# Fourteen tiles of the attention backward turned by DMA instead of by TensorE, with the buffers and the order that this needs

## The chip, the cores and the metric

The kernel runs on one NeuronCore of a Trainium2 chip. The metric is the device time of one execution in microseconds (us), from the profiler's clock. Three executions of the kernel before took 904.92, 905.37 and 907.75 us; their median is 905.37 us.

## The reference

What is computed is the forward output and all weight and input gradients of a gated mix of two branches on a sequence of 2048 tokens of width 512: `A`, attention with 32 heads of width 16 and a sliding window of 256 tokens, and `B`, a gated feed-forward of width 1376.

```python
g = sigmoid((x * gate_w).sum(-1, keepdims=True))
# A: qkv = x @ wqkv; scores = q k^T / 4, masked to 0 <= i - j < 256; p = softmax; o = p v
a = (o transposed back) @ wo
# B: gate = x @ W_gate; up = x @ W_up; gate = gate * (gate > 0)
b = (gate * up) @ W_down
out = g * a + (1 - g) * b
# returned: out, and by jax.vjp with grad_out the gradients of
# x (through A alone), wqkv, wo, W_gate, W_up, W_down, gate_w
```

All inputs and outputs are bfloat16.

## The kernel before

**Three stages.** The first (0 to about 250 us of the profile) is the feed-forward with its weight gradients. The second (250 to about 705 us) is the attention, forward and backward in one pass; the change lies here. The third (705 to 905 us) has two loops over the 16 token tiles: first the products with `W_down` and the gradient of `wo`, then the gradient of `x` and the output.

**Units of the attention.** The 32 heads are four *head groups* `c` = 0 to 3 of eight heads. The 2048 tokens are 16 tiles `j` of 128 queries, in four *token groups* `tg` of four tiles. A query tile sees three key tiles `kb`: its own (role `d`, masked along the diagonal), the one before (role `m`, unmasked) and the one two before (role `f`, the *far* tile, masked the other way). Four heads at a time (`half` 0 holds the even heads, `half` 1 the odd ones) make one *unit*: a 128 x 512 tile of probabilities. A head group has 90 units, all four have 360.

For each unit TensorE makes `ST` (line 688: scores of four heads, 128 x 512) and `dPT` (line 711: gradient of the probabilities). ScalarE takes the exponential of `ST` (line 697), GpSimd masks it if the role is `d` or `f`, and VectorE multiplies it with `dPT` (line 716). This gives two tiles, `Pu` and `Pd`. `rowsum` (lines 725 and 727) multiplies both, as they are, into `BA`. The products `CD` (`cd_piece`, lines 542 and 545), which give the gradients of the keys and values, need `Pu` and `Pd` *turned* (transposed in blocks of 128 x 128).

**How a unit is turned.** `flip` does it in one of two ways. Roles `d` and `m` are turned by DMA: the two halves of a tile lie in one buffer (`PPd`, `PPm`), and one DMA transpose from the queue of SyncE (SP) turns both, 128 x 2048 elements (line 744). Far units (and four `m` units at the end) are turned by TensorE: eight 128 x 128 transposes against the identity into `pt` (line 754), and then one copy of 128 x 1024 out of PSUM by ScalarE or VectorE, by turns (line 72 or 74; the tile is named `p`).

**The order of the work** is written out by hand: a loop over slots `n`, one unit entering in each. In slot `n` the kernel emits `ST` and the exponential of unit `n`, `dPT` of unit `n-1`, the product of VectorE for unit `n-2`, the DMA turn of unit `n-3`, and `rowsum` of unit `n-4` with its turn on TensorE, if it has one. Inside a slot, other work fills in:

- `cdq` holds the `CD` products with the slot from which each may run. When all units of query tile `j` are through `rowsum`, the six products of key tile `j-2` enter: those of older query tiles may run one slot later, those of tile `j` itself (the far units) five slots later. The queue is worked strictly in order.
- `prq` holds the six steps of `project_parts` for the next token group: projections Q and dO, the turn of these two by DMA (`rows`, line 181, 128 x 1024 elements), projections K and V, and `tr_kv`. A running `credit` (1.5 for a slot, less what each step costs) and a slot by which it is due decide when a step is emitted.
- `bgq` holds 16 pieces of `grad_parts`: the weight gradient of the head group before (line 642), four matmuls each, four pieces in a row to one PSUM tile. They enter at query tile 3 of the next head group, all together.
- `late` holds weight loads for the third stage (`plan`): among them the turns of `wqkv` by DMA (line 582) into the slot `p0`, after the projections of the fifth token group. `W_rest` is the list of the other weight turns for the third stage: four are issued at the end of the attention, one more at each pair of token tiles in the first loop of the third stage.

K and V (`K0`, `K1`, `V0`, `V1`, `KV1`) of a token group are read by the units of this group and of the first two query tiles of the next. Three sets of buffers hold them: one in the pool `pjA`, two in the pool `pj` (line 126 and line 519).

SP's queue, in order, issues the DMA turns of the attention, the stores of weight gradients (`ws`) and of `rows_st` (line 565), and the loads.

Of the kernel before, what the change touches and what calls it, by code (L numbers as in the profile page):

```python
# [11 lines left out]
BF = mybir.dt.bfloat16  # L12
# [10 lines left out]
def kernel(  # L23
# [20 lines left out]
    nc = tc.nc  # L44
    P = 128
# [9 lines left out]
    NT = S // P  # L55
# [42 lines left out]
    def slot(tag):  # L98
        return big.tile([P, DC, TGW], BF, tag=tag, name=tag)
# [12 lines left out]
    if True:  # L112
# [10 lines left out]
        def project_parts(c, tg):  # L123
            t4 = {}
            proj[(c, tg)] = t4
            pj = lambda: pjA if (c * NTG + tg) % 3 == 0 else pjs["b"]

            def mm(nm, which, eng):
                ps, tag, bufs, _, _ = pools["now"]
# [385 lines left out]
    if True:  # L515
        st = p3.enter_context(tc.tile_pool(name="attst", bufs=2))
        gwp = p3.enter_context(tc.tile_pool(name="gwp", bufs=2))
        p3b = ExitStack()
        pjs["b"] = p3b.enter_context(tc.tile_pool(name="pj", bufs=2))
        wk = p3b.enter_context(tc.tile_pool(name="attw", bufs=2))  # L520
        pps = ExitStack()
        ps = pps.enter_context(tc.tile_pool(name="attps", bufs=2, space=PSUM))
# [61 lines left out]
        def clear(name):  # L584
            nc.gpsimd.memset(W6[(name, FC - 1)][0:FC * P - F, :], 0.0)
# [32 lines left out]
        def load_gw():  # L618
            nc.sync.dma_start(gw_b[:], gate_w.partition_broadcast(P))

        plan = {2: [load_gw], 5: turns("wqkv", A_wqkv, 0, 4, "p0"), 7: turns("wqkv", A_wqkv, 4, 8, "p1"),
                11: turns("wqkv", A_wqkv, 8, 12, "p2"),
                12: turns("Wg", B_W_gate, 0, 4, "x0") + turns("Wg", B_W_gate, 4, 8, "d0"),
                15: loads("Wd", B_W_down, 0, "x3") + loads("Wd", B_W_down, 4, "d3") + loads("Wd", B_W_down, 8, "p3")}
        W_rest = (turns("Wg", B_W_gate, 8, 12, "x1") + [lambda: clear("Wg")] + turns("Wu", B_W_up, 0, 4, "d1") + turns("Wu", B_W_up, 4, 8, "x2")
                  + turns("Wu", B_W_up, 8, 12, "d2") + [lambda: clear("Wu")])

        def grad_parts(c, tail=False):
            out = []
# [26 lines left out]
                    out.append((lambda part=part, t0=t0, f=(t0 == 0), l=(t0 + 4 == NT): piece(part, t0, f, l), t0 + 4 < NT))  # L656
            return out

        class Unit:
            pass  # L660

        units = []
        for c in range(DC):
            for j in range(NT):
                kbs = [k for k in (j - 1, j, j - 2) if k >= 0]
                for half in range(2):
                    order = kbs if half or len(kbs) < 3 else [kbs[0], kbs[2], kbs[1]]
                    for ki, kb in enumerate(order):
                        u = Unit()
                        u.c, u.j, u.kb, u.half = c, j, kb, half  # L670
                        u.first = ki == 0 and half == 0
                        u.last = ki == len(kbs) - 1 and half == 1
                        u.role = ("d", "m", "f")[j - kb]
                        u.pair = u.role == "d" or (u.role == "m" and (c < DC - 1 or j < NT - 2))
                        u.own = u.role == "f"
                        u.dma = u.pair
                        units.append(u)
        NU = len(units)

        pairs = {}  # L680

        def front(u):
            tg, jl = u.j // TPG, u.j % TPG
            z = zt[(u.c * NTG + tg) % ZB]
            KTt = proj[(u.c, u.kb // TPG)][f"K{u.half}"]
            ksl = slice((u.kb % TPG) * P, (u.kb % TPG + 1) * P)
            ST = ps.tile([P, HH, P], F32, tag="M", bufs=4, name="ST")
            nc.tensor.matmul(ST[:], lhsT=KTt[:, ksl], rhs=z[:, 0, :, jl, :], start=True, stop=True)  # L688
            if not u.own:
                if u.half == 0:  # L690
                    tag = f"PP{u.role}"
                    pairs[(u.c, u.j, u.kb)] = wk.tile([P, 2, 2, HH, P], BF, tag=tag, bufs=3, name=tag)
                u.PP = pairs[(u.c, u.j, u.kb)][:, u.half, :, :, :]
                u.Pu, u.Pd = u.PP[:, 0, :, :], u.PP[:, 1, :, :]
            else:
                u.Pu = wk.tile([P, HH, P], BF, tag="Pu", bufs=2, name="Pu")
            nc.scalar.activation(u.Pu[:], ST[:], ACT.Exp)  # L697
            if u.role == "d":
                nc.gpsimd.affine_select(out=u.Pu[:], in_=u.Pu[:], compare_op=ALU.is_ge, fill=0.0, base=0,  # L699
                                        pattern=[[0, HH], [1, P]], channel_multiplier=-1)  # L700
            elif u.role == "f":
                nc.gpsimd.affine_select(out=u.Pu[:], in_=u.Pu[:], compare_op=ALU.is_ge, fill=0.0, base=-1,  # L702
                                        pattern=[[0, HH], [-1, P]], channel_multiplier=1)
# [7 lines left out]
            nc.tensor.matmul(u.dPT[:], lhsT=VTt[:, ksl], rhs=z[:, 1, :, jl, :], start=True, stop=True)  # L711

        def gradp(u):
            if u.own:
                u.Pd = wk.tile([P, HH, P], BF, tag="Pd", bufs=2, name="Pd")
            nc.vector.tensor_tensor(out=u.Pd[:], in0=u.Pu[:], in1=u.dPT[:], op=ALU.mult)  # L716

        def rowsum(u):
# [17 lines left out]
        def flip(u):  # L736
            key = (u.c, u.j, u.kb, "p2")
            if u.role != "f" and key not in P2 and not (u.pair and u.half == 0):
                P2[key] = wk.tile([P, 2, 2, HH, P], BF, tag=f"P2{u.role}", bufs=3, name=f"p2{u.role}")
            if u.dma:  # L740
                if u.pair and u.half == 0:
                    return
                hs = slice(0, 2) if u.pair else slice(u.half, u.half + 1)
                nc.sync.dma_start_transpose(out=P2[key][:, hs, :, :, :].rearrange("p b a h q -> p (b a h) q"),
                                            in_=pairs[(u.c, u.j, u.kb)][:, hs, :, :, :].rearrange("p b a h q -> p (b a h q)"))
                for b in range(2)[hs]:
                    P2[(u.c, u.j, u.kb, b)] = P2[key][:, b, :, :, :]
                return
            eng = ("act", "dve", "act")[copier["i"] % 3] if u.c == 0 else ("act", "dve")[copier["i"] % 2]
            copier["i"] += 1  # L750
            pt = psr.tile([P, 2, HH, P], BF, tag="TR", name="pt")
            for a, src in enumerate((u.Pu, u.Pd)):
                for hh in range(HH):
                    nc.tensor.transpose(pt[:, a, hh, :], src[:, hh, :], ident[:])  # L754
            p2 = P2[key][:, u.half, :, :, :] if u.role == "m" else wk.tile([P, 2, HH, P], BF, tag="P2f", bufs=4, name="p2")[:]
            evac(p2, pt[:], eng)
            P2[(u.c, u.j, u.kb, u.half)] = p2

# [84 lines left out]
        with tc.manual_schedule():  # L843
# [36 lines left out]
            while n <= NU + LAG or ev or cdq or bgq:  # L880
                now = ev.pop(n, [])
                u = units[n] if n < NU else None
                if u is not None:
                    gi = u.c * NTG + u.j // TPG
                    if u.first and u.j == 0:
                        sts[u.c] = st.tile([P, NT, 4, P], BF, tag="rows_st", name="rows_st")
                    if u.first and u.j % TPG == 0:
                        if gi + 1 < len(groups):
                            prq = project_parts(*groups[gi + 1]) if gi else second
                            due = n + sum(2 * min(3, j + 1) for j in range(u.j, u.j + TPG)) - 3  # L890
                            if gi + 2 == len(groups):
                                due -= 10
                    if u.first and u.j == TPG and ends:
                        copies.append(ends.pop(0))
                    if u.first and u.j == 1 and u.c > 0:
                        ready = grad_parts(u.c - 1)
                    if u.first and u.j == TPG - 1 and u.c > 0:
                        bgq += ready
                    front(u)
                    if u.last and gi + 1 == len(groups) and u.j % TPG in (1, 3):  # L900
                        ev.setdefault(n + 2, []).append(("dma", (lambda: load_a(0)) if u.j % TPG == 3 else lambda: load_h(0)))
# [18 lines left out]
                if w is not None:  # L920
                    rowsum(w)
                    if not w.dma:
                        flip(w)
                    if w.last:
                        for s, eng, f in small_ops(w.c, w.j, n - 2):
                            ev.setdefault(s, []).append((eng, f))
                        done = [w.j - 2] if w.j >= 2 else []
                        if w.j == NT - 1:
                            done += [NT - 2, NT - 1]
                        for kb in done:  # L930
                            qbs = range(kb, min(NT, kb + 3))
                            for qb in qbs:
                                for half in range(2):
                                    e = n + (1 if qb < w.j else 5)
                                    cdq.append((e, w.c, kb, qb, half, qb == qbs[-1] and half == 1))
                if v is not None and not (w is not None and w.first):
                    front_dp(v)
# [13 lines left out]
                elif held and credit > 0.3:  # L951
                    held = background()
                    credit -= 0.65
                elif prq and not held and ((credit > 0.4 and n > fed + 1) or due - n <= len(prq)):
                    fed = n
                    credit -= (0.44, 0.86, 0.86, 0.1, 0.86, 0.86)[len(prq) - 1]
                    prq.pop(0)()
# [3 lines left out]
                        ev.setdefault(n + 1, []).append(("dma", flush))  # L961
                    if not prq:
                        late += plan.get(gi + 1, [])
                elif bgq and len(prq) <= 2 and credit > 0.3:
                    held = background()
                    credit -= 0.65
                if u is not None and u.c == DC - 1 and not bgq and u.j > 6 and "grads" not in S2:
# [179 lines left out]
```

## Time and profile before

| | |
|---|---|
| median of three executions | 905.37 us |
| profiled execution: its time | 907.23 us |
| profiled execution: its span | 905.5 us |
| TensorE (PE) busy | 889.8 us, 98% of the span |
| VectorE (DVE), ScalarE (ACT), GpSimd (POOL) busy | 510.8, 445.6, 493.9 us |
| mean granted TensorE clock | 0.998 |
| turns of far units and others on TensorE (line 754) | 928 transposes (448 from `Pu`, 448 from `Pd`, 32 from `PPm`) |
| DMA turns (line 744) | 64 of `PPd`, 58 of `PPm` |

The span runs from the first to the last instruction of the core; the execution's time has some 1.7 us more around it. Matmuls overlap in the array, so the busy time of a line of TensorE, a sum of durations, is more than the time that it takes of the engine; what a matmul costs is read from the distance of the starts in the timeline.

### The profile page before, as it was taken

Reading aid. Unit: us, or ns where it says so; the run is one execution under the profiler, and the core shown is the slowest. Engines: PE = TensorE matmul, PEld = TensorE weight load, DVE = VectorE, ACT = ScalarE, POOL = GpSimd, SP = SyncE. Lnnn points to the kernel's source line nnn. Section 1 sums busy time; section 2 is a strip of 40 time slices with the busy share of each in tenths; the row PEclk is TensorE's granted clock in tenths of the full one; section 3 lists DMA queues with packets and bytes.
Section 4 is the critical chain, followed back from the end, with each engine's and each line's share of the span. In section 5 each row is a group of like instructions: output and inputs, shape, how many; then the busy total and the mean of one; then the engine's idle time right before and its main releaser. Section 6 shows DMA issues by size and latency. Waiting matters only on the chain.

```text
span 905.5 us, 25948 instructions
## 1 busy us (share of the span) xinstructions
PE 889.8 (98%) x10607; PEld 561.2 (62%) x10607; DVE 510.8 (56%) x946; ACT 445.6 (49%) x787; POOL 493.9 (55%) x937
## 2 busy tenths in 40 slices
PE   8999999999989999999999999999998999999998
PEld 5565665665657777667776677766676544444445
DVE  4433435434468887678886778876787101433343
ACT  6422223222278777667776677766787212111111
POOL 3654445445267778767877577876687200222232
PEclk9999999999999999999999999999999999999999
DMA  9989889999889999999999989999999999998940
GB/s 300 188 183 200 190 189 203 214 220 212 193 143 159 185 185 198 186 169 155 181 176 192 183 162 187 173 196 184 199 207 193 226 234 241 261 273 218 203 121 30
DMA packets 520984, 174.57 MB, mean 193 GB/s; under 512 B 446817, under 2 KB 519745, under 8 KB 520865
## 3 DMA queue, kind: packets, MB, share of 16 engines
q1 hardware_dynamic: 498624, 150.62, 89.6%
q10 hardware_dynamic: 20608, 17.70, 7.3%
q0 software_dynamic: 1632, 4.59, 1.4%
q8 instruction: 83, 1.36, 0.6%
q14 instruction: 37, 0.30, 0.1%
HBM read 34.37 MB, written 36.24 MB: 78 GB/s over the span
## 4 chain that ended last, share of the span: by engine, by line
PE 86%; DVE 5%; POOL 2%; ACT 2%; DMA 2%; issue 1%; SPq 1%; ACTq 0%; POOLq 0%; DVEq 0%
PE wps L412 8%; PE dxps L1049 8%; PE ST L688 7%; PE dPT L711 7%; PE pt L754 5%; PE dxps L1079 4%; PE gps L363 4%; PE dhps L363 4%; PE dps L414 4%; PE ups L363 4%; PE bps L1026 4%; PE pp L133 4%; PE BA L725 4%; PE CD L542 4%; PE wps L642 4%; PE BA L727 2%
## 5 line engine op out<-in xcount | busy, mean ns | idle before, releaser
L688 PE MATMUL ST<-z,K 128*128 128x512 bf16 x360 | 135.8, 378 | 3.3 <-ACT PPd L697 1.3
L711 PE MATMUL dPT<-z,V 128*128 128x512 bf16 x360 | 135.9, 378 | 1.8 <-DVE Pd L716 0.5
L699 POOL TENSOR_SCALAR_AFFINE_SELECT PPd<-PPd 128x512 bf16<-128x512 bf16 x128 | 81.7, 638 | 79.6 <-ACT PPd L697 79.3
L377 POOL TENSOR_TENSOR hT<-rg,upm 128x512 bf16<-128x512 bf16 x44 | 51.3, 1166 | 114.4 <-DVE upm L375 103.6
L412 PE MATMUL wps<-dgu_r,x_r 128*128 128x256 bf16 (+1 forms) x704 | 103.9, 270 | 0.0
L716 DVE TENSOR_TENSOR PPd<-PPd,dPT 128x512 bf16<-128x512 bf16 x128 | 86.9, 680 | 19.9 <-PE dPT L711 12.3
L702 POOL TENSOR_SCALAR_AFFINE_SELECT Pu<-Pu 128x512 bf16<-128x512 bf16 x112 | 72.3, 646 | 35.3 <-ACT Pu L697 34.2
L697 ACT ACTIVATE PPd<-ST 128x512 bf16<-128x512 f32 x128 | 77.0, 602 | 23.7 <-PE ST L688 18.8
L716 DVE TENSOR_TENSOR Pd<-Pu,dPT 128x512 bf16<-128x512 bf16 x112 | 76.4, 682 | 21.6 <-PE dPT L711 11.3
L412 PEld LDWEIGHTS <-x_r 128*128 128x128 bf16 x704 | 68.4, 98 | 30.8
L697 ACT ACTIVATE Pu<-ST 128x512 bf16<-128x512 f32 x112 | 67.4, 602 | 37.2 <-PE ST L688 37.1
L716 DVE TENSOR_TENSOR PPm<-PPm,dPT 128x512 bf16<-128x512 bf16 x120 | 80.1, 667 | 7.1 <-PE dPT L711 5.9
L697 ACT ACTIVATE PPm<-ST 128x512 bf16<-128x512 f32 x120 | 72.4, 603 | 17.2 <-PE ST L688 16.7
L375 DVE SCALAR_TENSOR_TENSOR upm<-rg,ups 128x512 bf16<-128x512 bf16 x44 | 30.1, 684 | 79.9 <-PE ups L363 42.1
L369 ACT ACTIVATE rg<-gps 128x512 bf16<-128x512 f32 x44 | 26.3, 597 | 88.8 <-PE gps L363 53.8
L414 PE MATMUL dps<-db_r,h_r 128*128 128x512 bf16 x176 | 66.7, 379 | 0.0
L72 ACT COPY p<-pt 128x1024 bf16<-128x1024 bf16 x59 | 60.1, 1019 | 4.2
L1061 ACT COPY a_sb<-aps 128x512 f32<-128x512 f32 x16 | 9.4, 586 | 106.9 <-issue 99.8
L387 POOL TENSOR_TENSOR dgu<-dh_sb,rg 128x512 bf16<-128x512 bf16 x44 | 57.9, 1315 | 5.3 <-ACT dh_sb L383 5.3
L642 PE MATMUL wps<-rows_st,x_r 128*128 128x384 bf16 x256 | 50.3, 325 | 0.0
L386 DVE TENSOR_TENSOR dgu<-dh_sb,upm 128x512 bf16<-128x512 bf16 x44 | 33.0, 749 | 29.9 <-ACT dh_sb L383 27.0
L133 PE MATMUL pp<-x,p 128*128 128x512 bf16 x192 | 49.0, 377 | 0.0
(178 smaller groups left out, 2327.9 us busy)
## 6 DMA issues: line engine op xcount, KB each, us to landing
dqkvo_d<-rows_st SPq DMA_DIRECT2D x15, 512.0 KB, 3.9
hT_d<-hT ACTq DMA_DIRECT2D x44, 128.0 KB, 2.8
dgT_d<-dgu ACTq DMA_DIRECT2D x44, 128.0 KB, 3.1
duT_d<-dgu ACTq DMA_DIRECT2D x44, 128.0 KB, 2.9
h<-hT_d SPq DMA_DIRECT2D x8, 640.0 KB, 5.1
dgT_g<-dgT_d SPq DMA_DIRECT2D x8, 640.0 KB, 5.2
duT_g<-duT_d SPq DMA_DIRECT2D x8, 640.0 KB, 6.4
go_g<-in_grad_out_dram SPq DMA_DIRECT2D x16, 256.0 KB, 4.7
```

The costliest lines, as they stand in the source:

```text
L133: nc.tensor.matmul(pp[:], lhsT=w_p[c][:, cd, which * P:(which + 1) * P], rhs=x_T[tg][:, cd, :], start=(cd == 0), stop=(cd == DC - 1))
L363: nc.tensor.matmul(out[:], lhsT=w(c), rhs=x(c), start=(c == 0), stop=(c == DC - 1))
L412: nc.tensor.matmul(acc["w"][:, c, 0:2 * nw], lhsT=x_r[:, t, c * P:(c + 1) * P], rhs=k.dgu_r[:, :, i, s0:P], start=(go_ and c % 2 == 0), st ...
L414: nc.tensor.matmul(acc["d"][:], lhsT=k.h_r[:, i, :], rhs=db_r[:, t, :], start=go_, stop=no_)
L642: nc.tensor.matmul(wps[:], lhsT=x_r[:, t, part * P:(part + 1) * P], rhs=sts[c][:, t, 0:3, :], start=first and t == t0, stop=last and t == ...
L688: nc.tensor.matmul(ST[:], lhsT=KTt[:, ksl], rhs=z[:, 0, :, jl, :], start=True, stop=True)
L697: nc.scalar.activation(u.Pu[:], ST[:], ACT.Exp)
L699: nc.gpsimd.affine_select(out=u.Pu[:], in_=u.Pu[:], compare_op=ALU.is_ge, fill=0.0, base=0, pattern=[[0, HH], [1, P]], channel_multiplier=-1)
L702: nc.gpsimd.affine_select(out=u.Pu[:], in_=u.Pu[:], compare_op=ALU.is_ge, fill=0.0, base=-1, pattern=[[0, HH], [-1, P]], channel_multiplier=1)
L711: nc.tensor.matmul(u.dPT[:], lhsT=VTt[:, ksl], rhs=z[:, 1, :, jl, :], start=True, stop=True)
L716: nc.vector.tensor_tensor(out=u.Pd[:], in0=u.Pu[:], in1=u.dPT[:], op=ALU.mult)
L1049: nc.tensor.matmul(to, lhsT=src[:, fc, lsl], rhs=W6[(wt, fc)][:, cols], start=(fc == 0 and wt == "Wg"), stop=False)
```

## The change

Six edits belong together.

1. **Fourteen far units go by DMA**: those of `half` 0 in head groups 1 and 2 (`FARC`) at query tiles 3, 4, 5, 6, 8, 9 and 10. `flip` issues one DMA transpose of 128 x 1024 for each on SP's queue, in the place where the pairs are turned, instead of eight transposes on TensorE and a copy.
2. **Buffers**: `Pu` and `Pd` of a far unit now lie in one tile, one of four named `PF`. In head groups 1 and 2 three of them rotate over `half` 0 and one is for `half` 1. The turned far tiles get five buffers instead of four, and in head groups 1 and 2 two more places in the slot `p0` (every third of a cycle of seven).
3. **CD of the far units** may run seven slots later instead of five in head groups 1 and 2.
4. **Two sets of K and V instead of three** (`pj` with one buffer). So K, V and `tr_kv` of the next token group wait for a gate: 12 slots into the group, or 5 if it begins a head group. In the last token group but one they are due four slots later than before.
5. **The weight gradient pieces** of head groups 0 and 1 enter in four quarters, at query tiles 3, 5, 9 and 13 of the next head group; those of head group 2 enter as before. They may run while K waits for its gate.
6. **The turns of the first four column blocks of `wqkv`** into `p0`, two DMAs, leave the attention and come at the end of `W_rest`, the clearing of `Wu` joined to its last turn. The list then has 11 entries instead of 10, and its last two fall to the sixth and seventh pair of token tiles in the third stage.

```diff
-            pj = lambda: pjA if (c * NTG + tg) % 3 == 0 else pjs["b"]
+            pj = lambda: pjA if (c * NTG + tg) % 2 == 0 else pjs["b"]
...
-        pjs["b"] = p3b.enter_context(tc.tile_pool(name="pj", bufs=2))
+        pjs["b"] = p3b.enter_context(tc.tile_pool(name="pj", bufs=1))
...
-        plan = {2: [load_gw], 5: turns("wqkv", A_wqkv, 0, 4, "p0"), 7: turns("wqkv", A_wqkv, 4, 8, "p1"),
+        plan = {2: [load_gw], 7: turns("wqkv", A_wqkv, 4, 8, "p1"),
...
-                  + turns("Wu", B_W_up, 8, 12, "d2") + [lambda: clear("Wu")])
+                  + turns("Wu", B_W_up, 8, 12, "d2"))
+        W_rest[-1] = lambda last=W_rest[-1]: (last(), clear("Wu"))
+        W_rest += turns("wqkv", A_wqkv, 0, 4, "p0")
...
+        FARC = (1, 2)
...
-                        u.dma = u.pair
+                        u.far = u.own and half == 0 and c in FARC and j in (3, 4, 5, 6, 8, 9, 10)
+                        u.dma = u.pair or u.far
...
+        PF = [wk.tile([P, 2, HH, P], BF, tag=f"PF{i}", bufs=1, name="PF") for i in range(4)]
+        far = {"in": 0, "out": 0}
+
+        def far_out(u):
+            i = far["out"]
+            far["out"] = (i + 1) % 7
+            if u.c in FARC and i % 3 == 2:
+                if "x" not in far:
+                    far["x"] = slot("p0")[:].rearrange("p k n -> p (k n)")
+                return far["x"][:, (i // 3) * 1024:(i // 3 + 1) * 1024].rearrange("p (a h q) -> p a h q", a=2, h=HH)
+            return wk.tile([P, 2, HH, P], BF, tag="P2f", bufs=5, name="p2f")[:]
...
-                u.Pu = wk.tile([P, HH, P], BF, tag="Pu", bufs=2, name="Pu")
+                if u.c in FARC:
+                    i = 3 if u.half else far["in"] % 3
+                    far["in"] += 1 - u.half
+                else:
+                    i = (2 * u.j + u.half) % 4
+                u.Pu, u.Pd = PF[i][:, 0, :, :], PF[i][:, 1, :, :]
+                u.PP = PF[i]
...
+            if u.far:
+                P2[(u.c, u.j, u.kb, u.half)] = p2 = far_out(u)
+                nc.sync.dma_start_transpose(out=p2.rearrange("p a h q -> p (a h) q"),
+                                            in_=u.PP[:].rearrange("p a h q -> p (a h q)"))
+                return
...
-            p2 = P2[key][:, u.half, :, :, :] if u.role == "m" else wk.tile([P, 2, HH, P], BF, tag="P2f", bufs=4, name="p2")[:]
+            p2 = P2[key][:, u.half, :, :, :] if u.role == "m" else far_out(u)
...
-                                due -= 10
+                                due -= 6
+                            gate = n + (12 if u.j else 5)
...
-                    if u.first and u.j == TPG - 1 and u.c > 0:
+                    if u.first and u.c in FARC and u.j in (3, 5, 9, 13):
+                        bgq += ready[:NT // 4]
+                        del ready[:NT // 4]
+                    if u.first and u.c > FARC[-1] and u.j == TPG - 1:
                         bgq += ready
...
-                                    e = n + (1 if qb < w.j else 5)
+                                    e = n + (1 if qb < w.j else 7 if w.c in FARC else 5)
...
-                elif prq and not held and ((credit > 0.4 and n > fed + 1) or due - n <= len(prq)):
+                elif prq and not held and (len(prq) > 3 or n >= gate) and ((credit > 0.4 and n > fed + 1) or due - n <= len(prq)):
...
-                elif bgq and len(prq) <= 2 and credit > 0.3:
+                elif bgq and (len(prq) <= 2 or len(prq) == 3 and n < gate) and credit > 0.3:
```

2 lines of the change are left out of this document (removed).

## The prediction, made before the changed kernel was run

> **What bounds the kernel now.** I read the page first: busy time of each engine, then the slices.
>
> ```profile
> span 905.5 us, 25948 instructions
> PE 889.8 (98%) x10607; PEld 561.2 (62%) x10607; DVE 510.8 (56%) x946; ACT 445.6 (49%) x787; POOL 493.9 (55%) x937
> ...
> PEclk9999999999999999999999999999999999999999
> DMA  9989889999889999999999989999999999998940
> ```
>
> TensorE is busy for 98% of the span at full clock, the other compute engines for about half. But the DMA row is at 9 nearly everywhere too, and the change moves work from the first to the second. So I cut the attention into its head groups: the second and third (367 to 591 us), which the change touches, the fourth (591 to 705), and the first loop of the third stage.
>
> ```profile
> core 0: us, PE busy (x) PEld busy (x) DVE busy (x) ACT busy (x) POOL busy (x), PEclk, DMA share, GB/s
> ...
> 367.00:479.00 112.00, 111.18 (x1944) 78.31 (x1941) 86.65 (x160) 80.57 (x143) 81.31 (x188) 1.00 1.06 177
> 479.00:591.00 112.00, 111.74 (x1964) 78.95 (x1961) 86.79 (x161) 80.56 (x144) 81.96 (x190) 1.00 1.07 177
> 591.00:705.00 114.00, 110.19 (x1972) 78.84 (x1969) 83.61 (x154) 80.10 (x143) 83.08 (x192) 1.00 1.13 194
> 705.00:780.00 75.00, 73.58 (x438) 35.67 (x437) 9.90 (x25) 14.88 (x27) 6.59 (x13) 1.00 1.02 236
> ```
>
> In head groups 1 and 2 TensorE lacks 0.8 and 0.3 us of 112, and VectorE, next, has 25 us to spare. In head group 3 TensorE idles 3.8 us. The DMA share counts packets in flight, which overlap (it exceeds 1), so it can't show what room is left. SP's queue and finer slices can:
>
> ```profile
> 422.04 1.39 SPq L181 DMA_TRANSPOSE rows<-zT  x1
> 423.54 3.12 SPq L744 DMA_TRANSPOSE p2m<-PPm  x1
> 426.77 1.82 SPq L744 DMA_TRANSPOSE p2d<-PPd  x1
> 428.72 2.67 SPq L744 DMA_TRANSPOSE p2m<-PPm  x1
> 431.49 3.18 SPq L744 DMA_TRANSPOSE p2d<-PPd  x1
> ```
>
> ```profile
> DMA  9900198909999999990499979999928999999009
> ...
> 420.00:447.00 27.00, 26.95 (x503) 19.44 (x502) 22.88 (x44) 20.79 (x38) 21.09 (x49) 1.00 1.13 178
> ```
>
> Here SP issues one turn behind the other. The slice row (420 to 447 us, 0.68 us a slice) has a few slices near 0, but mostly 9. So the DMA side is nearly full in dense stretches; even so TensorE is busy 26.95 of these 27 us. It is the bound, and the queue runs close behind.
>
> **The gain: transposes leave TensorE.** Its timeline shows one far turn, then the next matmul:
>
> ```profile
> 424.56 0.38 PE L754 MATMUL pt<-ident,Pu 128*128 128x128 bf16 x4
> 424.78 0.39 PE L754 MATMUL pt<-ident,Pd 128*128 128x128 bf16 x4
> 425.00 0.38 PE L711 MATMUL dPT<-z,V 128*128 128x512 bf16 x1
> ```
>
> From start to start, eight transposes take 0.44 us, 55 ns each. Fourteen turns are 14 x 0.44 = **6.2 us**, all on the path, since TensorE has no gap there to absorb them. The Trainium skill, page "TensorE: Matmul & The Clock Gate", section "Back-to-back issue gap", gives about 81 ns a matmul for a sustained stream of this width, and 56 ns as the isolated gap: by 81 the gain would be 112 x 81 ns = 9.1 us (an estimate). The trace agrees with the 56 (55 measured).
>
> ```profile
> L72 ACT COPY p<-pt 128x1024 bf16<-128x1024 bf16 x59 | 60.1, 1019 | 4.2
> ...
> L74 DVE COPY p<-pt 128x1024 bf16<-128x1024 bf16 x53 | 36.3, 685 | 11.4 <-PE pt L754 11.0
> ```
>
> Fourteen of these copies go too, about 7 us from ScalarE and 5 from VectorE. Neither is the bound: 0.
>
> **The cost: fourteen turns more for SP and the DMA engines.** No far turn by DMA is in the trace. The nearest row is the turn of Q and dO (line 181), which has the same 128 x 1024 elements; the other is half a pair's.
>
> ```profile
> L181 SPq DMA_TRANSPOSE rows<-zT x16: 1233/1258/1832, 232.7 to 654.6; - x16
> ...
> L744 SPq DMA_TRANSPOSE p2d<-PPd x64: 1755/2533/4056, 253.8 to 703.3; - x64
> L744 SPq DMA_TRANSPOSE p2m<-PPm x58: 1717/2942/5205, 258.3 to 691.8; - x58
> ...
> DMA to landing us min/median/max: 4.2/5.4/8.7
> ```
>
> ```profile
> 380.75 1.78 SPq L582 DMA_TRANSPOSE p<-in_A_wqkv_dram  x1
> ...
> 399.58 1.49 SPq L582 DMA_TRANSPOSE p<-in_A_wqkv_dram  x1
> ```
>
> Half a pair's turn is 1.27 to 1.47 us, line 181 has 1.26 and at most 1.83. I take 1.26, the same size. A head group has 16 `d` pairs and 15 `m` pairs: 16 x 2.53 + 15 x 2.94 = 84.6 us, with four turns of rows 89.6, with the two turns of `wqkv` (1.78 + 1.49) 92.9 of 112 us in head group 1. These two leave and seven far turns (8.8) come: 98.4 us. Head group 2 has no such relief there: 89.6 + 8.8 = 98.4. TensorE will need 112 - 3.1 = 108.9 us in each. The queue fits, stores included, though with less room.
>
> It fits only on average, so lateness decides. A far turn is issued in the slot three after its unit enters; with the product two slots later, its first `CD` comes 12 slots on. A slot lasts 112/90 = 1.24 us, so 15 us remain, against a landing of 5.4 us, at most 8.7. Pairs have 11 slots. So I cost the added turns at 0; without the cover, each late one stalls TensorE by what it is late. The quarters of `grad_parts` help: their 64 matmuls now lie at query tiles 3, 5, 9 and 13, so tiles 9 to 14, where the queue above ran solid, get longer in TensorE time.
>
> **Waits that move.** (a) Head group 3 has two stalls behind loads for the third stage:
>
> ```profile
> PE CD L542 <- DMA p2m<-PPm: 1.1, 1, 1.1
> ...
> PE ST L688 <- ACT PPd L697: 1.0, 1, 1.0
> ```
>
> ```profile
> 667.21 0.57 SPq L607 DMA_DIRECT2D x<-in_B_W_down_dram  x1
> 667.85 0.52 SPq L607 DMA_DIRECT2D d<-in_B_W_down_dram  x1
> 668.41 0.51 SPq L607 DMA_DIRECT2D p<-in_B_W_down_dram  x1
> 669.03 5.21 SPq L744 DMA_TRANSPOSE p2m<-PPm  x1
> ...
> 678.37 4.74 SPq L744 DMA_TRANSPOSE p2m<-PPm  x1
> ```
>
> Three loads go ahead of a pair's turn, which takes 5.21 us to issue instead of 2.94, and products of the next tile wait. Worked through the loop slot by slot, the last K, V and `tr_kv` move from slots 6, 8, 10 of their token group to 12, 13, 14, ahead of these loads, which start two slots later. So some 2.2 us of TensorE work comes between the turns of tile 9 and the loads, and only two loads precede that turn. The stalls (2.1 us) should shrink: from 2.1 gained to 1 lost; I take **1.0 gained**.
>
> (b) The last `CD` of head groups 1 and 2 comes at slot 15 of the next head group instead of 13, just ahead of the fourth piece of `grad_parts`, which reads its copy. This is a new wait of TensorE, in order, at two places:
>
> ```profile
> L548 ACT CAST rows_st<-CD 128x256 bf16<-128x256 f32 x64 | 23.9, 373 | 18.7 <-PE CD L545 18.6
> ```
>
> A copy is 0.37 us, with an exponential (0.6) ahead about 1 us; three matmuls of the piece cover half of it. 0 to 2.0 us for both; I take **0.5 lost**.
>
> (c) K and V in two sets: the gate opens when the last reader of `ST` has been emitted, so the writes of K wait on VectorE for nothing that is not done. At the last token group the three steps are in consecutive slots, and the first write of `KV1` (GpSimd) waits for a `rowsum` of the next slot; masks queue behind it. 0 to 1.0; I take **0.4 lost**.
>
> (d) Two `wqkv` turns go into the third stage, the second ahead of the loads for the second loop:
>
> ```profile
> 764.90 5.69 SPq L840 DMA_TRANSPOSE turned<-dqkvo_d  x1
> ...
> turned<-dqkvo_d SPq DMA_TRANSPOSE x1, 7.7
> ```
>
> ```profile
> 773.94 0.59 PE L1058 MATMUL aps<-wo_z,turned 128*128 128x512 bf16 x2
> ```
>
> `turned` lands at 772.6 and is needed at 773.94: 1.3 us in hand, and a turn ahead takes 1.5 to 1.8. 0 to 1.3 lost; **0.3**, since SP stands idle just before.
>
> (e) At 0: SP waits some two slots longer at the start of head groups 2 and 3, where a `d` turn reuses a buffer that the later `CD` still reads; rows and pairs queue behind, and 11 slots cover it. The `PF` tiles are free again before they are written; the fifth far buffer and `p0` only give room.
>
> **Sum**: 6.2 + 1.0 - 0.5 - 0.4 - 0.3 = 6.0 us. From the profiled execution (907.23 us; span 905.5) this makes 901.2. That execution was 1.9 us over the median of 905.37, which I take as its own disturbance: **899.4 us**. By the bounds: 6.2 + 2.1 = 8.3 gained gives 897.1; 6.2 - 1 - 2.0 - 1.0 - 1.3 = 0.9 gained gives 904.5.
>
> **Rivals.** *The queue becomes the bound* (slower). If what SP idles can't be used, since it waits there for data in order, each added turn lengthens the chain: 14 x 1.26 less the relief of 3.3 = 14.3, and TensorE's 6.2 is hidden: 919.7 us. For it: the solid stretch above. Against it: TensorE's 26.95 of 27 us in that stretch. It decides once the backlog, landings included, passes 11 slots (13.6 us; now at most 8.7). The Trainium skill, page "Perfetto Trace Analysis", section "What 'DMA-bound' means", counts a kernel as DMA-bound where the issuing sequencer's track is solid DMA slices; by that rule this rival would win. The trace so far disagrees, by the same 26.95. Chance 0.10.
>
> *Stalls eat the gain.* (b), (c) and (d) at their bounds leave 1 to 4 us: 901.3 to 904.4 us. For it: four waits get tighter at once; against: each has a cover. Chance 0.18.
>
> *Two sets of K and V are too few*: ten token groups with a gate, each with TensorE or VectorE held for one write of K:
>
> ```profile
> L169 DVE TENSOR_SCALAR K<-KT,par 128x512 bf16<-128x512 bf16 x14 | 6.3, 492 | 0.1
> ```
>
> 10 x 0.49 = 4.9 us, which leaves about 1 us: 904.3. Against it: the gate lies behind the readers. Chance 0.05. *The change doesn't do what it says*, so that no transposes leave: 905.4, chance 0.02.
>
> **How the numbers follow.** The forecast has 0.65. About 0.3%, 2.7 us, is what a measurement of this kernel can tell from no change. Faster by more: 0.65 and two thirds of the second rival, 0.77. Within: the rest of it, the third and the fourth, 0.12. Slower: 0.11, nearly all the queue. The range takes in the bounds of the sum, 897.1 to 904.5, and below them 0.5 us, by which the two lower executions before differ (904.92 and 905.37): 896.6 to 904.5; the queue's 919.7 and what lies beyond stays out.
>
> **What would show it.** Right: TensorE with 10495 matmuls; 816 transposes on line 754's successor; head groups 1 and 2 at about 109 us each, TensorE still above 99% in them; no wait of `CD` on a far turn. Wrong: waits of TensorE on a DMA in head groups 1 and 2, with turns landing more than 11 us after issue; a gap before the fourth weight gradient piece; idle time before the first `aps`; head group 3 longer than 114 us.

## The result and the profile after

The changed kernel takes **911.32 us** (median of seven runs, 909.84 to 916.02) against 905.37 of the kernel before in the same comparison: ratio 1.0063, 95% interval 1.0048 to 1.0078. The forecast was 899.4. The profiled execution took 910.74 us, span 909.0 (before 907.23 and 905.5).

The page of the changed kernel:

```profile
span 909.0 us, 25632 instructions
PE 882.8 (97%) x10408; PEld 555.5 (61%) x10495; DVE 501.8 (55%) x939; ACT 435.0 (48%) x780; POOL 492.7 (54%) x937
...
q1 hardware_dynamic: 513408, 154.29, 92.7%
...
L779 PE MATMUL pt<-ident,PF 128*128 128x128 bf16 x784 | 59.5, 218 | 0.0
```

TensorE's weight loads are 10607 - 112 = 10495, and 784 transposes from `PF` with 32 from `PPm` make the 816 expected: the work left TensorE. (Line 779 is the successor of line 754; `ST` is now line 704, the exponential 719, `dPT` 733, the product of VectorE 736, the far turn by DMA 762, the pair's turn 769.) TensorE is busy 7.0 us less, in a span 3.5 us longer. The stretches, cut as in the prediction, say where:

```profile
367.00:479.00 112.00, 110.56 (x1907) 76.86 (x1915) 85.59 (x164) 76.64 (x144) 83.06 (x194) 1.00 1.18 192
479.00:591.00 112.00, 108.44 (x1888) 75.79 (x1894) 82.58 (x158) 75.43 (x140) 80.72 (x189) 1.00 1.19 190
591.00:705.00 114.00, 109.31 (x1944) 78.02 (x1948) 81.24 (x148) 79.18 (x141) 82.45 (x191) 0.99 1.14 195
705.00:780.00 75.00, 72.69 (x444) 35.91 (x449) 9.08 (x24) 14.55 (x28) 5.60 (x13) 1.00 1.04 235
```

By the column of PE (the one behind the length) TensorE idles 1.4 and 3.6 us in head groups 1 and 2, where it lacked 0.8 and 0.3. The DMA share rose by 0.12 in both.

**An account by head groups.** I take the distance from one `ST` to the next, slot by slot, and subtract what the matmuls emitted in that slot take back to back. The rest is TensorE's loss:

| head group | time before | after | difference | loss before | loss after |
|---|---|---|---|---|---|
| 0 | 101.9 | 103.9 | +2.0 | 4.2 | 6.2 |
| 1 | 115.5 | 113.0 | -2.5 | 0.8 | 1.5 |
| 2 | 115.9 | 115.3 | -0.6 | 1.2 | 3.7 |
| 3 | 115.2 | 119.3 | +4.1 | 4.3 | 8.2 |
| sum | 448.5 | 451.5 | +3.0 | 10.4 | 19.5 |

The matmul work went from 438.1 to 432.0 us: 6.1 us less, as forecast. The losses rose by 9.1. After the attention 0.9 us more comes on top, and the first stage is 0.4 us shorter, which together make the 3.5 us of the spans.

**Where the loss sits.** The waits of TensorE in head groups 1 and 2, first after, then before:

```profile
PE dPT L733 <- ACT PPd L719: 1.4, 2, 0.9
PE wps L644 <- ACT rows_st L548: 0.7, 1, 0.7
PE CD L542 <- ACT rows_st L548: 0.4, 2, 0.2
PE dPT L733 <- ACT PPm L719: 0.3, 1, 0.3
PE ST L704 <- ACT PPd L719: 0.2, 1, 0.2
```

```profile
PE ST L688 <- DVE PPm L716: 0.6, 1, 0.6
```

No `CD` waits for a DMA here, which is what I had told the reader to look for. TensorE waits for exponentials into `PPd`. Their own waits, in the list of ScalarE over the attention, first after, then before:

```profile
ACT PPd L719 <- DMA p2d<-PPd: 11.7, 9, 2.5
```

```profile
ACT PPd L697 <- DMA p2d<-PPd: 2.3, 1, 2.3
```

So an exponential can't write because a turn is still reading the buffer. One of the nine, with SP's queue ahead of it, and then ScalarE and TensorE, in the timeline:

```profile
534.39 0.59 SPq L636 DMA_DIRECT2D out_dram<-ws  x1
535.08 0.57 SPq L565 DMA_DIRECT2D dqkvo_d<-rows_st  x1
535.74 1.80 SPq L762 DMA_TRANSPOSE p<-PF  x1
537.63 2.29 SPq L181 DMA_TRANSPOSE rows<-zT  x1
540.02 2.78 SPq L769 DMA_TRANSPOSE p2m<-PPm  x1
542.90 3.00 SPq L769 DMA_TRANSPOSE p2d<-PPd  x1
...
548.22 0.60 ACT L719 ACTIVATE PPd<-ST 128x512 bf16<-128x512 f32 x1 [1.53 <-DMA p2d<-PPd]
...
548.87 0.38 PE L733 MATMUL dPT<-z,V 128*128 128x512 bf16 x1 [0.49 <-ACT PPd L719]
```

The turn at 542.90 is that of query tile 8. VectorE had finished its data at 530.8; it was issued 12.1 us later, since SP had others ahead, each starting about 0.1 us after the one before had ended. There are three buffers of `PPd`, so tile 11 writes the same one: its exponential waits until the turn lands, and `dPT` waits for the exponential. The first `CD` on this turn comes at 551.3, after that.

For the whole stretches I added up the distances between SP's DMA issues that are over 0.25 us (SP free), and took the largest start delay of a turn in each head group, from the end of VectorE's product to the issue:

| | SP free in 367-479 | 479-591 | 591-697 | start delay, group 1 | group 2 | group 3 |
|---|---|---|---|---|---|---|
| before | 17.6 us | 14.2 | 1.5 | 4.7 | 5.3 | 10.1 |
| after | 0.7 us | 0.0 | 0.3 | 7.4 | 12.6 | 12.6 |

SP's free time is gone, the delay grows through head groups 1 and 2, and head group 3 begins with 7.0 us of it instead of 3.3. There the weight loads come, and `CD` waits:

```profile
687.39 0.21 PE L542 MATMUL CD<-rq,p2m 128*128 128x32 bf16 x1 [1.53 <-DMA p2m<-PPm]
```

### The profile page after: what moved, and what is told of

It reads as the page before. It is cut to its first block, busy times and chain, and to the rows that moved or that the text cites. A ratio compares the mean times of both kernels' runs of the same rounds, so it can differ in the third digit from the quotient of the medians.

```text
span 909.0 us, 25632 instructions
## 1 busy us (share of the span) xinstructions
PE 882.8 (97%) x10408; PEld 555.5 (61%) x10495; DVE 501.8 (55%) x939; ACT 435.0 (48%) x780; POOL 492.7 (54%) x937
## 4 chain that ended last, share of the span: by engine, by line
PE 79%; DMA 8%; ACT 4%; SPq 3%; POOL 2%; DVE 2%; issue 1%; ACTq 0%; POOLq 0%
PE ST L704 7%; PE wps L412 7%; PE dPT L733 7%; PE dxps L1078 7%; PE pt L779 4%; PE pp L133 4%; PE dxps L1108 4%; PE CD L542 4%; PE dhps L363 4%; PE BA L745 4%; PE wps L644 4%; PE gps L363 4%; PE ups L363 3%; PE dps L414 3%; PE bps L1055 3%; DMA p2d<-PPd 2%
## 5 line engine op out<-in xcount | busy, mean ns | idle before, releaser
L412 PE MATMUL wps<-dgu_r,x_r 128*128 128x256 bf16 (+1 forms) x704 | 103.9, 270 | 1.4 <-DVE wst L74 0.6
L724 POOL TENSOR_SCALAR_AFFINE_SELECT PF<-PF 128x512 bf16<-128x512 bf16 x112 | 73.1, 653 | 27.5 <-ACT PF L719 26.0
L736 DVE TENSOR_TENSOR PF<-PF,dPT 128x512 bf16<-128x512 bf16 x112 | 76.4, 682 | 17.1 <-PE dPT L733 7.7
L719 ACT ACTIVATE PF<-ST 128x512 bf16<-128x512 f32 x112 | 68.1, 608 | 31.6 <-PE ST L704 30.9
L414 PE MATMUL dps<-db_r,h_r 128*128 128x512 bf16 x159 | 60.3, 379 | 0.0
L779 PE MATMUL pt<-ident,PF 128*128 128x128 bf16 x784 | 59.5, 218 | 0.0
L72 ACT COPY p2f<-pt 128x1024 bf16<-128x1024 bf16 x47 | 48.2, 1025 | 1.4
```

Source lines behind the costliest of these rows:

```text
L412: nc.tensor.matmul(acc["w"][:, c, 0:2 * nw], lhsT=x_r[:, t, c * P:(c + 1) * P], rhs=k.dgu_r[:, :, i, s0:P], start=(go_ and c % 2 == 0), st ...
L414: nc.tensor.matmul(acc["d"][:], lhsT=k.h_r[:, i, :], rhs=db_r[:, t, :], start=go_, stop=no_)
```

## The experiments

Two questions were open: what each part of the change costs, and whether the cost of the far turns is one of SP, of the buffers or of the number of turns. The ratios are against the kernel before on the same chip: 906.63 us for e1 to e4, 906.39 for e5 to e8, 907.16 for e9 to e11. The groups ran on different chips, so runs of different groups are compared by their ratios first.

**e1: everything but the far turns.**

```diff
-                        u.far = u.own and half == 0 and c in FARC and j in (3, 4, 5, 6, 8, 9, 10)
+                        u.far = u.own and half == 0 and c in FARC and j in ()
```

> The changed kernel with all far units turned by TensorE again; two sets of K and V, the quarters of the weight gradient, the later CD products, the buffers and the two late wqkv turns stay. Theory A (the rearrangement costs, the far turns by DMA gain): 911.3 + 6.2 less 1 to 3 us of stalls behind the fuller queue = 914.5 to 916.5 us, and head group 3 and head group 0 as slow as in the changed kernel (119 and 104 us). Theory B (the queue of the fourteen added turns is what costs): 905 to 907 us, head groups 0 and 3 back at 102 and 115 us.

909.29 us, ratio 1.0024 (1.0010 to 1.0039), which lies between the two theories and fits neither. The rearrangement alone costs about 2 us; losses by head group are 6.2, 0.6, 0.8 and 3.1 us. So head group 0's loss belongs to edits 2 to 6, and what head groups 1 to 3 lose more in the changed kernel comes with the far turns. The losses add up to 10.7 us, though, hardly more than the 10.4 before: in the profiled execution (910.67 us, 1.4 over the median) the attention takes 448.7 us from the first `ST` to the last, against 448.5 before. What it takes longer lies behind the attention, 211.1 us from the last `ST` to the end against 206.8. There `aps` waits 2.0 us for `turned` (edit 6), and the clock is at half for 3.4 us right after (last section); a load of `dgT_g` makes TensorE wait 1.0 us.

**e2: two sets of K and V alone** (edit 4, on the kernel before).

```diff
-        pjs["b"] = p3b.enter_context(tc.tile_pool(name="pj", bufs=2))
+        pjs["b"] = p3b.enter_context(tc.tile_pool(name="pj", bufs=1))
...
+                            gate = n + (12 if u.j else 5)
```

> The kernel before with edit 4 alone: two sets of K and V, the gate, and the due slot of the last group. Theory A: 905.4 + 2.0 (VectorE short in query tiles 5, 9 and 13 of head group 0) + 1 to 2 (the same once, and the loads of the third stage, in head group 3) + 0 to 2 (query tiles 5, 9 and 13 of head groups 1 and 2) = 909 to 911 us. Theory B: 904.5 to 906 us, no difference.

911.68 us, 1.0057 (1.0039 to 1.0075), a little above theory A. TensorE's waits over the attention:

```profile
PE ST L688 <- DVE PPm L716: 4.7, 8, 0.6
```

These were 1.2 us, two times, before. Without the pieces in quarters to fill the gate's slots, VectorE is late at each token group. Losses: 6.2, 2.7, 3.1, 4.4; in e1, with the quarters, head groups 1 and 2 lost 0.6 and 0.8.

**e3: the far turns alone** (edit 1 on the kernel before, three sets of K and V, `CD` after five slots; three `PF` tiles and three for the turned ones, which is what fits).

```diff
+                        u.far = u.own and half == 0 and c in FARC and j in (3, 4, 5, 6, 8, 9, 10)
+                        u.dma = u.pair or u.far
...
+            return wk.tile([P, 2, HH, P], BF, tag="P2f", bufs=3, name="p2f")[:]
```

> The kernel before with edit 1 alone, the same fourteen far units by DMA, in the room that the far tiles had: three tiles for Pu and Pd instead of two pairs' worth, three for the turned tiles instead of four. Three sets of K and V, CD after five slots, weight gradient pieces and wqkv turns as before. Theory A: 905.4 - 6.2 + 0 to 1.5 = 899.2 to 900.7 us. Theory B: 905 to 912 us, with TensorE waiting on DMA in head groups 1 and 2.

911.7 us, 1.0052 (1.0030 to 1.0074). The far turns alone lose as much as the whole change. With fewer buffers the `PF` tiles are late too:

```profile
PE dPT L722 <- ACT PF L708: 3.7, 4, 2.1
PE dPT L722 <- ACT PPd L708: 2.5, 2, 1.9
PE ST L696 <- ACT PPd L708: 1.9, 2, 1.6
PE CD L542 <- DMA p2m<-PPm: 1.7, 1, 1.7
```

**e4: VectorE's spread copies three slots apart** (on the changed kernel).

```diff
-ev.setdefault(n + 1 + k, []).append(("dve", lambda gi=gi, k=k: spread(gi + 1, k)))
+ev.setdefault(n + 1 + 3 * k, []).append(("dve", lambda gi=gi, k=k: spread(gi + 1, k)))
```

> The changed kernel with the four copies of VectorE that spread Q and dO into z (line 120) placed three slots apart instead of in four slots in a row. Theory A, its part on VectorE: the losses in query tiles 3, 5, 9 and 13 of head group 0 and 9 of head group 3 go, 911.3 - 2 to 3.5 = 908 to 909.5 us. Theory B: 911.3 us as it was, since the wait is for DMA.

910.49 us, 1.0041 (1.0025 to 1.0057), slower than theory A gave. The loss of head group 0 falls from 6.2 to 4.5 and the wait of `ST` for VectorE is gone from it. What is seen in the changed kernel without this edit is, on VectorE and then on TensorE:

```profile
333.54 0.64 DVE L736 TENSOR_TENSOR PPm<-PPm,dPT 128x512 bf16<-128x512 bf16 x1
334.21 0.42 DVE L120 COPY z<-zT 32x1024 bf16<-32x1024 bf16 x1
334.66 0.69 DVE L736 TENSOR_TENSOR PPd<-PPd,dPT 128x512 bf16<-128x512 bf16 x1
335.38 0.52 DVE L120 COPY z<-zT 32x1024 bf16<-32x1024 bf16 x1
```

```profile
334.24 0.38 PE L704 MATMUL ST<-z,K 128*128 128x512 bf16 x1 [0.58 <-DVE PPm L736]
```

A copy and a product in each slot come to about 1.2 us, more than such a slot has. The wait for VectorE is explained by this. What of the 1.7 us arrives at the end is not clear of noise: against the changed kernel it is 2.0 us by the ratios and 0.8 by the medians, and the intervals overlap. Head group 3's `CD` waits grow to 3.7 us.

**e5: e3 without issuing the fourteen turns.** TensorE's work is that of e3.

```diff
-                P2[(u.c, u.j, u.kb, u.half)] = p2 = far_out(u)
-                nc.sync.dma_start_transpose(out=p2.rearrange("p a h q -> p (a h) q"),
-                                            in_=u.PP[:].rearrange("p a h q -> p (a h q)"))
+                P2[(u.c, u.j, u.kb, 0)] = P2[(u.c, u.j - 1, u.kb - 1, 1)]
```

> The kernel of the far-alone run with the fourteen DMA turns left out: these units are turned by nobody, and their CD products read the turned far tile of the query tile before. So TensorE has lost the transposes and SP's queue has gained nothing. Theory Q (the queue of SP and the DMA engines has no room for the added turns): 906.6 - 6.2 + 0 to 1 = 900.4 to 901.5 us, backlog of the queue as before (pairs start 0.3 to 5 us after their data in head groups 1 and 2). Theory P (TensorE's transposes were not on the path, something else sets the pace of head groups 1 and 2): 905 to 907 us.

902.57 us, 0.9964 (0.9950 to 0.9978), about 1 us above what theory Q gave. Against e3 that is 8.0 us by the ratios and 9.1 by the medians: the price of fourteen turns on the queue, **some 0.6 us each**, while the work that leaves TensorE is worth 3.8 us here. The changed kernel against e1 agrees: losses of 19.5 us against 10.7, 0.63 us for each turn. SP is free for 12.3 and 8.5 us in the two stretches.

**e6: eight far turns, at query tiles 3 to 6** (e3 with a shorter list).

```diff
+                        u.far = u.own and half == 0 and c in FARC and j in (3, 4, 5, 6)
```

> The far-alone kernel with far turns by DMA at query tiles 3, 4, 5 and 6 alone, eight units. There the weight gradient pieces of the kernel before lengthen the tiles to about 9 us, and SP's queue has gaps. Theory Q: gain 8 x 0.44 = 3.5 us, less 0 to 1 us: 903 to 904.2 us; backlog in head groups 1 and 2 at most 5 us from query tile 8 on. A theory by which each far turn costs the same wherever it stands (5.1 + 6.2 = 11.3 us for fourteen, 0.8 us each): 906.6 - 3.5 + 6.4 = 909.5 us.

904.1 us, 0.9979 (0.9967 to 0.9991): faster than before, by about 2 of the 3.5 us that leave TensorE. TensorE's waits in head groups 1 and 2 are down to two:

```profile
PE ST L696 <- DVE PPm L725: 0.6, 1, 0.6
PE dPT L722 <- ACT PPd L708: 0.3, 1, 0.3
```

SP is still free for 4.8 and 2.4 us there, and losses are those of the kernel before (4.1, 0.9, 1.3, 4.1).

**e7: e3 with the stores taken off SP.**

```diff
-            eng = nc.gpsimd if (c == DC - 1 and t0 + TPG == NT) else nc.sync
+            eng = nc.gpsimd if (c == DC - 1 and t0 + TPG == NT) else nc.scalar
```

(and the stores of `ws` likewise)

> The far-alone kernel with the stores of rows_st and of the weight gradients (eight a head group, about 0.6 us of SP each) issued from ScalarE's queue instead of SP's. If SP's time to issue is what is full: about 5 us a head group of room, the backlog of head groups 1 and 2 falls from 6 to 10 us to 2 to 5 us, and 911.7 becomes 903 to 906 us. If the DMA engines are what is full (the bytes and packets stay): backlog and time stay, 910 to 912.5 us.

911.27 us, 1.0056 (1.0040 to 1.0072), no change from e3 in time. But the loss has moved. SP is free for 6.1 and 3.2 us in the two stretches where e3 has 0.4 and 0.0, and the largest delay falls from 8.0 to 6.8 us in head group 1 and from 10.3 to 7.7 in head group 2. Exponentials into `PF` wait 1.4 us for a turn instead of 5.6 (those into `PPd` 8.9 instead of 7.7), and TensorE's waits for exponentials into `PF` and `PPd` fall from 8.8 us to 3.0. Its waits for products of VectorE rise from 1.1 us to 5.7, because the stores now hold up ScalarE's queue, and an exponential behind them comes late:

```profile
PE ST L696 <- DVE PPm L725: 3.2, 6, 0.7
```

```profile
417.49 0.54 ACTq L634 DMA_DIRECT2D out_dram<-ws  x1
...
418.13 0.60 ACTq L634 DMA_DIRECT2D out_dram<-ws  x1
418.76 0.66 ACTq L565 DMA_DIRECT2D dqkvo_d<-rows_st  x1
419.47 0.60 ACT L708 ACTIVATE PPd<-ST 128x512 bf16<-128x512 f32 x1 [1.26 <-PE BA L736]
```

So the time alone would say that room on SP's queue doesn't help. The trace shows that it did help against the late turns, and that other waits took its place. Whether SP's issuing or the transfers behind it set the limit, this run doesn't settle.

**e8: twenty-eight far turns** (e3 with query tiles 2 to 15).

> The far-alone kernel with all 28 far units of half 0 of head groups 1 and 2 by DMA, twice as many. Theory Q: the backlog goes on growing, to 15 us and over, and every added turn costs more than the 0.44 us that it saves: 915 to 925 us, with waits of TensorE for DMA in head groups 1 and 2 themselves. If the loss of the far-alone run came from single places (the end of head group 3, the clock): 906 to 911 us, with 6 us more saved.

929.23 us, 1.0253 (1.0235 to 1.0271), beyond what theory Q gave. TensorE's work is 12.3 us less than before, its losses 32.9 us more. The waits:

```profile
PE dPT L722 <- ACT PF L708: 14.2, 7, 3.1
PE dPT L722 <- ACT PPd L708: 5.8, 4, 3.9
```

**e9: eight far turns, at query tiles 9 to 12.**

```diff
-                        u.far = u.own and half == 0 and c in FARC and j in (3, 4, 5, 6)
+                        u.far = u.own and half == 0 and c in FARC and j in (9, 10, 11, 12)
```

> The kernel before with eight far units by DMA as in the run with query tiles 3 to 6 (904.1 us), but at query tiles 9 to 12. The same TensorE work leaves (8 x 0.44 = 3.5 us). Theory Q (the backlog of the queue decides, and it grows over a head group): tiles 9 to 12 are where turns already start latest in the kernel before (up to 4.7 us after their data in head group 1, 5.3 in head group 2, and head group 3 begins with 3.3), so the lateness is carried into the next head group and the gain is lost: 907 to 912 us, with waits of CD on DMA in head groups 1 to 3. Rival N (only the number of turns decides, as long as the mean load fits): as with tiles 3 to 6, 904 us.

914.8 us, 1.0079 (1.0062 to 1.0096): with the same number of turns as e6, some 10 us slower, and more than theory Q gave. SP is free here for 12.8 and 10.8 us, more than in e6, but nearly all of it at query tiles 5 to 9, and none from tile 10 on; in e6 what is free lies at tile 9 and, the most of it, at tile 13, where the backlog can be worked off. The delay rises to 9.7 us at tile 12 of head group 1, enters head group 2 with 4.7 and head group 3 with 7.0 us. At the change of head group, where query tiles have two and four units and the three buffers of `PPd` come round sooner, it is paid:

```profile
478.82 2.40 SPq L758 DMA_TRANSPOSE p2d<-PPd  x1
479.37 0.60 ACT L708 ACTIVATE PPd<-ST 128x512 bf16<-128x512 f32 x1 [3.90 <-DMA p2d<-PPd]
...
480.02 0.38 PE L722 MATMUL dPT<-z,V 128*128 128x512 bf16 x1 [2.78 <-ACT PPd L708]
```

So the number alone doesn't decide (rival N falls). `CD` waits for a DMA in head group 3 alone (3.3 us), not in head groups 1 and 2 as I had expected there.

**e10: the changed kernel with far turns at tiles 3 to 6 only.**

> The changed kernel with far units by DMA only at query tiles 3 to 6 (eight instead of fourteen), everything else as changed. Theory Q: the losses of head groups 1 and 2 return to about those of the changed kernel without far turns (0.6 and 0.8 us), head group 3's to some 3 to 4 us, head group 0 keeps its 6 us (two sets of K and V); 909.3 - 3.5 = 905.8 us, at most 907.5. Rival A (the rearrangement of K, V and pieces is incompatible with any far turn, for VectorE's crowded slots then meet late turns): 908 to 911.

909.31 us, 1.0022 (1.0009 to 1.0036): above the 905.8 to 907.5 that theory Q gave, and in the range of rival A. Rival A's mechanism, VectorE's crowded slots meeting late turns, is not what the trace shows, though. Head groups 1 and 2 came out as Q said (losses 1.0 and 1.2), head group 0 as well (6.1), but head group 3 lost 6.5 us instead of 3 to 4. Of that, 3.4 us are two waits of `CD` for a turn. The start delay in head group 2 is 10.9 us against 7.5 in e6, and 5.6 goes over into head group 3 against 4.2. The rearrangement thus leaves less room for the same turns. I did not separate which of its parts does it; the quarters of `grad_parts`, which take TensorE work out of the tiles 4 and 6 to 8, are my guess.

**e11: e6, and one `m` pair of head group 3 turned by TensorE**, the one that goes behind three loads.

```diff
-                        u.pair = u.role == "d" or (u.role == "m" and (c < DC - 1 or j < NT - 2))
+                        u.pair = u.role == "d" or (u.role == "m" and (c < DC - 1 or j < NT - 2 and j != 9))
```

> The run with eight early far units (904.1 us), and one m pair of head group 3 (query tile 9, the one that goes behind the three loads and takes 6.4 us to issue) turned by TensorE: 16 transposes more, 0.9 us of TensorE. Theory Q: the two waits of CD on that queue (2.5 us together in the profile of the run with eight) shrink by more than that: 902.0 to 903.7 us. Rival: the wait only moves to the next turn behind the loads, and the 0.9 us come on top: 904.5 to 905.5 us.

**902.71 us, 0.9951 (0.9933 to 0.9969)**, the fastest of all, of those that leave nothing out. In head group 3 no `CD` waits for a DMA any more:

```profile
PE dPT L722 <- DVE PF L725: 0.5, 1, 0.5
PE CD L542 <- ACT rows_st L548: 0.5, 1, 0.5
```

Giving work *back* to TensorE there gains 1.4 us against e6 by the medians and 2.5 by the ratios, whose intervals just touch; in the profiles head group 3 is 1.7 us shorter. It is the same trade as the change, in the other direction, at a place where the queue is full.

## Why the prediction was wrong

**The gain, 6.2 us: right.** The work is 6.1 us less.

**"The queue fits, stores included": the step that failed.** I summed 98.4 us of turns against 108.9. Three things were missing. The stores and the 0.1 us between issues: SP's issues in 479 to 591 us before come to 93.8 us and the short distances to 4.0, not to 89.6. A far turn is not 1.26 us but 1.69 on the mean in head group 1 and 1.55 in head group 2. And the pairs of head group 2 take 86.6 us together, not 84.6 (before it was 83.3); e5, which issues no far turn, has 85.9, so it isn't shown that the far turns do this. After the change, issues and distances in that stretch come to 107.2 and 4.8 us: all of the 112 us, where TensorE would have needed 108.9. I had also tested the fit on the mean over a head group, where e6 and e9 show that it is the place that counts.

**"Lateness decides, and 15 us remain against a landing of at most 8.7": wrong twice.** The 8.7 us run from issue to landing; the delay ahead of the issue (up to 5.3 us in head groups 1 and 2 before, 10.1 in head group 3) belongs to it. And what a late `d` turn holds up first is not its reader, the `CD`. The 11 slots hold for an `m` pair. By the loop, the first `CD` of a `d` pair comes 15 slots after the slot of its turn, but the exponential that writes the source buffer again comes after 13: it follows 18 slots (three query tiles) after the one that wrote the buffer, and five of these are gone when the turn can be issued. At the change of head group, where tiles are shorter, 7 or 8 slots are left. In the example above the exponential came 3 us ahead of the `CD`. That is the wait that appeared in head groups 1 and 2, with none of `CD` on a DMA. Cost: 0.7 + 2.5 us of loss there, and the backlog handed to head group 3.

**(a) Head group 3: 1.0 gained; measured 3.9 lost.** I moved K and V ahead of the loads and left out that the queue would arrive with 7.0 us in it. Without the far turns (e1) the loss did fall, from 4.3 to 3.1, so the step held by itself.

**(c) Two sets of K and V: 0.4 lost; measured about 3**, 2.0 in head group 0 and 1.0 at query tile 9 of head group 3. I looked for a wait of the writes of K and found none; the cost is in VectorE's four spread copies, which now fall into successive slots (e2, e4).

**(b) right in size**: TensorE waits 0.7 us for `rows_st` at a fourth piece, in head group 2 alone, against 0.5 taken for two places. The order by itself doesn't make this wait: e1 and e10 have the same order, with none or eight of the far turns, and don't show it. **(d)** 0.3 taken, up to 1.3 allowed; `turned` is late by 1.1 us (and by 2.0 in e1, 1.2 in e4 and in e10; in no run without edit 6):

```profile
769.29 5.88 SPq L865 DMA_TRANSPOSE turned<-dqkvo_d  x1
```

```profile
777.28 0.60 PE L1087 MATMUL aps<-wo_z,turned 128*128 128x512 bf16 x2 [1.08 <-DMA turned<-dqkvo_d]
```

The sum of what was measured: 6.1 - 3.2 - 2.9 - 3.0 - 0.9 = 3.9 lost ((a) without the 1.0 us counted in (c); (b) lies in the 3.2), and 0.4 us back from the first stage gives the 3.5 us.

**The rival** "the queue becomes the bound" had the right cause and the wrong size: it made 919.7 us, because it let every added turn lengthen the chain by its whole issue time. The price is some 0.6 us a turn (e5); that SP's free time absorbs the rest is my reading of the table of SP's free time. I argued against it with TensorE's 26.95 busy us of 27 in a dense stretch. That number says that the buffers covered the queue *then*; it says nothing of the room left. The Trainium skill, page "Perfetto Trace Analysis", section "What 'DMA-bound' means", takes a solid track of the issuing sequencer as the sign; here it was the better sign, as the table of SP's free time shows. The same section names the transfer engines and the sequencer as two different limits; e7 doesn't tell them apart. Also open is whether a fourth buffer of `PPd` would have covered the delay, since no run tried it.

## What to carry to other kernels

Before giving a full engine's work to a queue, list that queue's idle time by place, and carry the backlog forward: a turn added where idle time follows costs little, one added where the next dense stretch follows is paid there (e6 against e9: some 10 us for the same eight turns). The deadline of a late transfer is the first instruction that touches any of its buffers, the source for writing as well as the result for reading, counted from the moment the data is ready and not from the issue. And an engine that is 100% busy next to a solid queue proves only that the slack has been enough so far.

## What the hardware showed that I had not expected

TensorE's granted clock fell to half for 3.4 us at waits that were, but for one, shorter than that. In the changed kernel, the stretches around the wait of 1.53 us above:

```profile
683.90:687.30 3.40, 1.78 (x40) 1.25 (x36) 2.05 (x4) 2.57 (x5) 2.68 (x8) 1.00 1.02 219
687.40:690.80 3.40, 3.40 (x46) 1.96 (x47) 1.25 (x2) 1.19 (x2) 1.11 (x4) 0.50 1.60 172
```

The half-clock window follows one in which TensorE was busy for 1.78 of 3.40 us. It is so at twelve places of other runs: e8 has six (1.05, 1.41, 0.42, 1.55, 1.31 and 0.53 us busy in the window ahead), e3 two (1.68, 1.54), e9 two (1.48, 0.69), e1 and e4 one each (1.36, 1.66). The waits there were 1.6 to 3.1 us long; the one of 3.9 us, in e8, was followed by half clock for twice as long. The Trainium skill, page "TensorE: Matmul & The Clock Gate", section "Why this matters for your kernels", warns of idle gaps above some 3 us; here about half a window of idling was enough. Half clock for 3.4 us costs at most 1.7 us of work, so a stall of 1.5 us can cost as much again; part of head group 3's loss is this. It did not follow every such stall: of the 21 waits of TensorE over 1.4 us from the attention on, in all the traces, 13 have it, and e10 has a wait of 2.3 us with no such window near it.
